# Attention scores in blocks of a triangle, one rescaling for the last rows, and a new list of shifts, in a fused scan and two-layer kernel

## The chip, the core and the metric

The kernel runs on one core of one Trainium2 chip, in one launch. The metric is device time in microseconds (us), from the start of the program to its end; smaller is better. TensorE is PE in the rows, with PEld for its weight loads; VectorE is DVE, ScalarE is ACT, GpSimd is POOL, and SyncE (SP) issues most of the DMA transfers.

## What is computed

The inputs x, a, B and C have 4 batches, 8 heads and 768 positions; a head has 32 values and a state of 16. A decayed linear attention goes first, cut to what matters:

```python
log_a = np.log(np.clip(a, 1e-06, 1.0))
for c in range(nc):                                # chunks of positions
    cum = np.cumsum(la, axis=-1)
    L = np.exp(cum[:, :, :, None] - cum[:, :, None, :]) * causal
    M = np.einsum('bhin,bhjn->bhij', Cc, Bc) * L   # scores, lower triangle
    y = M @ xc + (Cc @ state) * exp(cum)
    state = decay_full * state + sum_j (Bc_j x xc_j) * decay_from_j
```

Its 3072 rows of 256 values then pass two layers, each `h = x @ w_in` (256 to 2048), a function of h, and `g @ w_out` (2048 to 256). The first layer's function is ELU, the second's is Mish. All is float32.

## The kernel before

**Tiles.** The kernel takes chunks of T = 96 positions, not the reference's 32. With 8 chunks and 4 batches there are 32 tiles of the attention, numbered i = 4 x chunk + batch. A tile's scores for its 8 heads are 96x96 matrices with j on the partitions and i on the columns, so what counts is j up to i, and the rest is set to zero by the decay matrix `d` that they are multiplied with.

**Scores.** Tiles 0 to 7 (`TR0 = range(8)`) go the first way: C and B are transposed on TensorE in float32 (`at_tr0`, L699, four transposes), copied out, and multiplied in float32 by `at_scores0` (L739, 16 rows deep); one tile has eight of these matmuls in two blocks. Later tiles go the second way: ACT and DVE split B and C into three bfloat16 parts each (`at_split_1` to `at_split_4`, L610 to L627), one DMA transposes them (`at_split_5`, L631), and `at_scores` (L753) does one 96x96x96 matmul a head, four heads in each of two PSUM banks of the tag "s". `at_p` (L759) multiplies each bank into `d`. `at_y` (L791) then multiplies by x, head by head into 32 PSUM partitions each, two tiles at a time, and `at_st` (L828) makes the state's increment.

**Layers.** The rows are cut into blocks of 256 to 512 (`BL`), and each layer's 2048 inner values into 16 pieces. To hold float32 precision each product is made of three matmuls of high and low parts: L873 to L875 for h, L936 to L938 and L967 to L969 for the outputs. The first pieces of layer one use L941. The very last block of layer two (`LAST`) has its rows as PSUM partitions: `emit_y2` makes, for each group k of 128 rows, a matmul of 512 columns (L1006: the high part of g with high and low weights, in two halves of the bank) and one of 256 (L1007: the low part with the high weights, into half 0). `y2_out1` (L1022) scales half 1 into the result, `y2_out2` (L1027) scales half 0 and adds it, and `y2_store` (L1040) stores, part from SP's queue and part from ACT's.

**Weights.** The weights come as float64, in 32 loads of 512 KB; `job_1` to `job_5` (L391 to L434) make each into the high and low parts that the matmuls take.

**What sets the order.** The code does not issue instructions where it stands. Each piece is a `step` with one or more engines, a cost in us, and what it depends on. `run_steps` plans them all: it works a latest start for each step back from deadlines, adds to it what the table `SHIFT` has under the step's number, and then takes, engine by engine, the ready step with the earliest latest start. The instructions are emitted in the order so planned, and each engine runs its own list in that order. PSUM banks and other buffers are rings; `take` hands out the next place in one and notes who must be done with it.

Of the kernel before, what the change touches and what calls it, by code (L numbers as in the profile page):

```python
# [7 lines left out]
F32 = mybir.dt.float32  # L8
# [5 lines left out]
ALU = mybir.AluOpType  # L14
# [4 lines left out]
def tile_chain(  # L19
# [12 lines left out]
    nc = tc.nc  # L32
# [11 lines left out]
    DFF = w_in1.shape[1]  # L44
    NF = DFF // 128
    FP = 2
    EARLY = 10.0
    NP = NF // FP
    LAG = 5
    N0 = 8  # L50
    TR0 = range(8)

    ROWS = dict(zip(range(1, 4), (12, 13, 14, 15, 12, 14, 15)))
    WB, GB, HB, ND = 3, 3, 2, 3
# [32 lines left out]
    def early(step_k, cost):  # L87
# [2 lines left out]


    SHIFT = {
# [6 lines left out]
    }  # L99

    lock = set()
# [647 lines left out]
    def at_scores(i, half):  # L749
        s = s_t[i, half] = px.tile([T, H // 2, T], F32, tag="s", name="s")  # L750
        for k in range(H // 2):
# [2 lines left out]
                out=s[:, k, :], lhsT=bct[i, "b"][0:T, h, :], rhs=bct[i, "c"][0:T, h, :], start=True, stop=True  # L754
            )

    def at_p(i, half):
        hs = slice(half * (H // 2), (half + 1) * (H // 2))
        nc.vector.tensor_tensor(  # L759
            out=d_t[i][0:T, hs, :], in0=s_t.pop((i, half)), in1=d_t[i][0:T, hs, :], op=ALU.mult  # L760
        )
# [234 lines left out]
    def emit_y2(s, k):  # L996
        f = s % NF
        if f == 0:
            p, t = (pa, "acc") if k < 2 else (px, "s")
            acc[2, LAST, k] = p.tile([128, 2, DM], F32, tag=t, name="acc")  # L1000
        _, _, gh, gl = st[s]
        w = wt["o2", f // FP]
        y = acc[2, LAST, k]
        ts = slice(k * 128, k * 128 + 128)
        yk = y.rearrange("p z (k e) -> p z k e", k=2)
        nc.tensor.matmul(out=yk, lhsT=gh[:, ts], rhs=w[:, :, :, f % FP, :], start=(f == 0), stop=False)  # L1006
        nc.tensor.matmul(  # L1007
            out=yk[:, 0], lhsT=gl[:, ts], rhs=w[:, 0, :, f % FP, :], start=False, stop=(f == NF - 1)
        )
# [4 lines left out]
    def y2_out1(k, eng):  # L1014
        if k % 2 == 0:
            tl["oo", k] = at.tile([128, 2, DM], F32, tag="x", name="o", bufs=3)
        o = tl["o", k] = tl["oo", k - k % 2][:, k % 2]
        a, b = in_rows(acc[2, LAST, k][:, 1], o)
        if eng == V:
            nc.vector.tensor_scalar_mul(b, a, 1.0 / WS)  # L1020
        else:
            nc.scalar.activation(out=b, in_=a, func=AF.Copy, scale=1.0 / WS)  # L1022
# [72 lines left out]
    for j, (key, k) in enumerate(jobs):  # L1095
        rn, pn = [], []
        if j >= NJ:
            rn, pn = (w_free[j + 1 - NJ] if j + 1 < 2 * NJ else []), w_free[j - NJ]
            rf = []
            if j + 1 < 2 * NJ:  # L1100
                w_free[j + 1 - NJ] = rf
        else:
            rf = w_free[j]
            if key == "o1":
                w0_free[k] = rf
        q0 = step((DQ, 0.58, lambda j=j: load_job(j), 1.75), rn, rows_f.get(j, []))
        q1 = step(alt(lambda e, j=j: job_1(j, e), (V, 0.335), (A, 0.557)), q0)
        lock.add(q1)
        q2 = step((A, 0.552, lambda j=j: job_2(j)), q0)
        table[q2] = "exp"  # L1110
        q3 = step((V, 0.602, lambda j=j: job_3(j)), q1, q2)
        lock.add(q3)
        q4 = step(alt(lambda e, j=j: job_4(j, e), (A, 0.558), (V, 0.335)), q3, pn)
        q5 = step(alt(lambda e, j=j: job_5(j, e), (G, 1.27), (V, 0.603)), q4,
                  dl=slot_time(order.index((2, 0)) * NF + k * FP) + 10.0 if j >= NJ else 1e9)
        lock.update((q4, q5))
        rf.append(q5)
        raw_f = rf
        w_ready[key, k] = [q4, q5]
        LW.append(q0)  # L1120
        if key == "o1":
            w_ready["o0", k] = [q3]
# [56 lines left out]

    def two_scores(i, a5, tf, ex):  # L1180
        pz = []
        two = [take("s") for _ in range(2)]
        sc = step((PE, 0.43, lambda: [at_scores(i, z) for z in range(2)]), a5, [n for _, n in two])
        tf.append(sc)
        for z in range(2):
            pz.append(step((V, 0.47, lambda z=z: at_p(i, z)), sc, ex[z]))
            two[z][0].append(pz[-1])
        return pz
# [68 lines left out]
    for i in range(NB, tiles):  # L1257
        c, b = divmod(i, NB)
        if i % 2 == 0:
            bcf, bcn = take("bc")  # L1260
            lb = step((DQ, 1.15, lambda i=i: load_bc(i), 1.4), bcn)
            ys_dep, d_of = [], []
        d_f, d_n = take("d")
        d_of.append(d_f)
        if i in ROWS:
            lc, ex = rows_steps(i, d_n)
        else:
            lc = step((DQ, 0.52, lambda i=i: at_cumrow(i), 1.2), s_q4[c], d_n)
        cold = i in TR0
        if cold:  # L1270
            pf, pn = take("s")
            tr = step((PE, 0.40, lambda i=i: at_tr0(i)), lb, pn)
            tf, tn = take("t")
            a2 = step(alt(lambda e, i=i: at_tr0_out(i, e), (A, 0.372), (V, 0.47)), tr, tn)
            pf.append(a2)
        else:
            a2, a5, tf = three_parts(i, lb)
        if i not in ROWS:
            mk = step((G, 0.85, lambda i=i: at_mask(i)), lc)
            dd = []  # L1280
            for g in range(2):
                f = lambda e, i=i, g=g: at_diff(i, g * H // 2, (g + 1) * H // 2, e)
                dd.append(step(alt(f, (G, 0.80), (V, 0.47)), mk, s_q6))
                lock.add(dd[-1])
            ex = step((A, 0.735, lambda i=i: at_exp(i)), dd)
            table[ex] = "exp"
            ex = [ex, ex]
        csf, csn = take("cs")
        cs = step((G, 0.372, lambda i=i: at_cs(i)), lb, csn, s_d4)
        rc = step((V, 0.97, lambda i=i: at_rc(i)), cs, lc)  # L1290
        csf.append(rc)
        rc2 = step(alt(lambda e, i=i: at_rc2(i, e), (V, 0.37), (A, 0.52)), rc)
        lock.add(rc2)
        bcf += [a2, cs]
        if c + 1 < NCH:
            bf, bn = take("bw")
            b1 = step((G, 0.372, lambda i=i: at_bw_1(i)), lb, s_d3, bn)
            b2 = step((G, 0.372, lambda i=i: at_bw_2(i)), s_d7, b1)
            bcf.append(b1)
            ys_dep += [b1, b2]  # L1300
            d_of.append(bf)
        if cold:
            pz = []
            for z in range(2):
                two = [take("s"), take("s")]
                sc = step((PE, 0.52, lambda i=i, z=z: at_scores0(i, [z])), a2, [n for _, n in two])
                tf.append(sc)
                pz.append(step((V, 0.535, lambda i=i, z=z: at_p0(i, z)), sc, ex[z]))
                for pf, _ in two:
                    pf.append(pz[-1])  # L1310
        else:
            pz = two_scores(i, a5, tf, ex)
        ys_dep += [pz, rc, rc2]
        if i % 2 == 0:
            continue
        i -= 1
        pf, pn = take("s")
        parts, cost = [lambda i=i: at_y(i, 2)], 1.0
        if c + 1 < NCH:
            parts.append(lambda i=i: at_st(i))  # L1320
            cost = 1.2
        y = step((PE, cost, lambda parts=parts: [f() for f in parts]), ys_dep, LX[i], pn, SO[i - NB])
        oy = out_of_y(i, 2, y)
        if c + 1 < NCH:

            SO[i] = step((V, 1.2, lambda i=i: at_st_out(i)), y, LX[i + NB], list(YHI[i].values()))
            pf.append(SO[i])
        for f in d_of:
            f.append(y)
        pf += oy  # L1330
        xf[i].append(y)
# [93 lines left out]
    for f, k in [(f, k) for f in range(NF - 2) for k in range(NK)] + [(f, k) for k in range(NK) for f in (NF - 2, NF - 1)]:  # L1425
        s, ydep, gf, lf, ydl = last[f]
        y = step((PE, 0.347, lambda s=s, k=k: emit_y2(s, k)), ydep, four[k][1] if f == 0 else [], y, dl=ydl)
        gf.append(y)
        lf.append(y)
        if f == NF - 1:  # L1430
            if k % 2 == 0:
                _, on = take("x")
            o = step(alt(lambda e, k=k: y2_out1(k, e), (A, 0.27), (V, 0.33)), y, on)
            o = step((V, 0.35, lambda k=k: y2_out2(k)), o)
            step((DQ, 1.0, lambda k=k: y2_store(k), 0.48), o)
    run_steps()

# [29 lines left out]
```

## Time and profile before

| | us |
|---|---|
| median of three timed runs | 598.0 (597.68 to 598.23) |
| the profiled execution | 597.4 |
| its span, first to last instruction | 595.7 |
| PE busy | 585.2 |
| DVE busy | 427.6 |
| ACT busy | 363.2 |
| POOL busy | 133.1 |

The span is what lies between the first and the last instruction that the profiler recorded; the execution's own time has the launch's ends besides. Busy times are those of one execution, and an engine that is busy is not for that reason the one that others wait for; which one that is, the chain of waits tells, followed back from the last instruction. A matmul's row shows when it started and a modelled length that is longer than the step to the next one, since matmuls overlap: costs on PE are read from starts.

### The profile page before, as it was taken

To read this page: it belongs to the slowest core of one execution; us is meant where nothing else is said; L and a number is where in the kernel's file an instruction comes from. 1 tells how busy PE (TensorE), PEld (TensorE's weight loads), DVE (VectorE), ACT (ScalarE), POOL (GpSimd) and SP (SyncE) were. 2 spreads that over 40 slices of the span, in tenths; PEclk is the share of its full clock that TensorE was granted. 3 is DMA by queue.
4 is the path that set the end of the run, shared out by engine and by line. 5 is a ranking of instruction groups with operands and counts; after the bars stand their busy time and mean duration, and the time that the engine had idled before them with its cause. 6 is when DMAs were issued, how large, how long until landed. Compare 5 with 4: busy or idle time off the path is not lost.

```text
span 595.7 us, 10184 instructions
## 1 busy us (share of the span) xinstructions
PE 585.2 (98%) x3648; PEld 490.1 (82%) x3648; DVE 427.6 (72%) x941; ACT 363.2 (61%) x668; POOL 133.1 (22%) x200
## 2 busy tenths in 40 slices
PE   6999999999999999999999999999999999999997
PEld 5777999998888888888888788888888888888885
DVE  5898989999737889988776878665655665443443
ACT  4799999987615887777456796544543444322321
POOL 2455564340201245352005233000020000000000
PEclk9599999999999999999999999999999999999999
DMA  7999899310113656651015451100310000000101
GB/s 147 237 254 240 206 295 247 80 28 2 14 22 67 111 104 121 127 113 12 0 28 100 71 110 27 29 8 3 72 28 1 22 15 1 1 0 1 35 2 36
DMA packets 136279, 44.86 MB, mean 75 GB/s; under 512 B 124820, under 2 KB 125332, under 8 KB 136228
## 3 DMA queue, kind: packets, MB, share of 16 engines
q1 hardware_dynamic: 135876, 43.92, 33.7%
q8 instruction: 28, 0.46, 0.3%
q10 hardware_dynamic: 352, 0.30, 0.2%
q14 instruction: 23, 0.19, 0.1%
HBM read 31.48 MB, written 3.29 MB: 58 GB/s over the span
## 4 chain that ended last, share of the span: by engine, by line
PE 95%; DMA 2%; SPq 1%; DVE 1%; issue 0%; ACT 0%; POOL 0%; DVEq 0%; POOLq 0%
PE h L873 15%; PE h L874 15%; PE h L875 15%; PE acc L936 7%; PE acc L937 7%; PE acc L938 7%; PE acc L967 6%; PE acc L968 6%; PE acc L969 6%; PE acc L1006 3%; PE ys L791 2%; PE acc L941 2%; PE s L753 1%; PE acc L1007 1%; DMA t<-stk 1%; PE s L739 1%
## 5 line engine op out<-in xcount | busy, mean ns | idle before, releaser
L873 PE MATMUL h<-xyh,wi 128*128 128x512 f32 (+2 forms) x416 | 159.9, 384 | 0.0
L874 PE MATMUL h<-xyl,wi 128*128 128x512 f32 (+2 forms) x416 | 156.3, 376 | 0.0
L875 PE MATMUL h<-xyh,wi 128*128 128x512 f32 (+2 forms) x416 | 155.9, 375 | 0.0
L916 DVE TENSOR_TENSOR gl<-w,gh 128x512 fp32r<-128x512 f32 (+2 forms) x179 | 121.1, 678 | 21.8 <-ACT gh L417 13.2
L920 ACT ACTIVATE w<-h 128x512 f32<-128x512 f32 x96 | 57.0, 598 | 111.7 <-PE h L875 93.4
L419 DVE CAST gh<-w 128x512 fp32r<-128x512 f32 (+2 forms) x102 | 42.7, 419 | 75.6 <-PE acc L968 45.0
L873 PEld LDWEIGHTS h<-xyh,wi 128*128 128x128 f32 x416 | 78.9, 190 | 14.0 <-DVE g L905 0.3
L875 PEld LDWEIGHTS h<-xyh,wi 128*128 128x128 f32 x416 | 78.9, 190 | 12.9
L874 PEld LDWEIGHTS h<-xyl,wi 128*128 128x128 f32 x416 | 79.0, 190 | 11.8 <-DVE xyl L811 0.4
L889 ACT ACTIVATE w<-h 128x512 f32<-128x512 f32 (+2 forms) x104 | 55.9, 545 | 43.7 <-PE h L875 28.9
L936 PE MATMUL acc<-gh,wo 128*128 128x512 f32 (+2 forms) x208 | 75.8, 364 | 0.0
L937 PE MATMUL acc<-gh,wo 128*128 128x512 f32 (+2 forms) x208 | 74.9, 360 | 0.0
L938 PE MATMUL acc<-gl,wo 128*128 128x512 f32 (+2 forms) x208 | 74.9, 360 | 0.0
L417 ACT ACTIVATE gh<-w 128x512 fp32r<-128x512 f32 (+2 forms) x98 | 57.5, 592 | 27.5 <-PE acc L937 21.0
L967 PE MATMUL acc<-gh,wo 128*128 128x512 f32 x160 | 62.9, 393 | 0.0
L968 PE MATMUL acc<-gh,wo 128*128 128x512 f32 x160 | 62.3, 389 | 0.0
L969 PE MATMUL acc<-gl,wo 128*128 128x512 f32 x160 | 62.3, 389 | 0.0
L916 POOL TENSOR_TENSOR gl<-w,gh 128x512 fp32r<-128x512 f32 (+2 forms) x21 | 23.3, 1110 | 146.8 <-PE s L753 97.0
L897 DVE TENSOR_SCALAR w<-w 128x512 f32<-128x512 f32 (+2 forms) x71 | 28.6, 407 | 29.5 <-ACT w L889 29.2
L905 DVE TENSOR_TENSOR w<-h,w 128x512 f32<-128x512 f32 (+2 forms) x71 | 44.1, 626 | 1.6
L936 PEld LDWEIGHTS acc<-gh,wo 128*128 128x128 f32 x208 | 39.2, 188 | 5.5
L937 PEld LDWEIGHTS acc<-gh,wo 128*128 128x128 f32 x208 | 39.2, 188 | 5.1
(119 smaller groups left out, 865.5 us busy)
## 6 DMA issues: line engine op xcount, KB each, us to landing
raw<-in_moe_w_in_dram SPq DMA_DIRECT2D x16, 512.0 KB
raw<-in_moe_w_out_dram SPq DMA_DIRECT2D x16, 512.0 KB
d<-cum_d SPq DMA_DIRECT2D x28, 288.0 KB
xs<-in_x_dram SPq DMA_DIRECT2D x14, 192.0 KB
out_dram<-turned SPq DMA_DIRECT2D x80, 32.0 KB
bc<-in_C_dram SPq DMA_DIRECT2D x14, 96.0 KB
bc<-in_B_dram SPq DMA_DIRECT2D x14, 96.0 KB
xs<-in_x_dram SPq DMA_DIRECT2D x4, 96.0 KB
```

The source lines that it names most:

```text
L417: nc.scalar.activation(out=out, in_=in_, func=AF.Copy)
L873: nc.tensor.matmul(out=h, lhsT=hi[:, k, fs], rhs=xh[:, k, :], start=(k == 0), stop=False)
L874: nc.tensor.matmul(out=h, lhsT=hi[:, k, fs], rhs=xl[:, k, :], start=False, stop=False)
L875: nc.tensor.matmul(out=h, lhsT=lo[:, k, fs], rhs=xh[:, k, :], start=False, stop=(k == 1))
L916: alu(eng).tensor_tensor(out=gl, in0=w, in1=gh.bitcast(F32), op=ALU.subtract)
L920: nc.scalar.activation(out=new_w(s), in_=st[s][0], func=AF.Mish)
L936: nc.tensor.matmul(out=y, lhsT=hi[:, f % FP, ds], rhs=gh, start=(f == 0), stop=False)
L937: nc.tensor.matmul(out=y, lhsT=lo[:, f % FP, ds], rhs=gh, start=False, stop=False)
L938: nc.tensor.matmul(out=y, lhsT=hi[:, f % FP, ds], rhs=gl, start=False, stop=(f == NF - 1))
L967: nc.tensor.matmul(out=y, lhsT=hi[:, k], rhs=gh, start=(f == 0), stop=False)
L968: nc.tensor.matmul(out=y, lhsT=lo[:, k], rhs=gh, start=False, stop=False)
L969: nc.tensor.matmul(out=y, lhsT=hi[:, k], rhs=gl, start=False, stop=(f == NF - 1))
```

## The change

**Scores.** From tile 12 on (`TRI = 12`) `two_scores` calls `at_scores_tri` and `at_p_tri`. A head's 96x96 block is cut into its first 64 rows, with all 96 columns (`low`), and its last 32 rows with the last 32 columns (`high`); the piece that is left out lies wholly on the masked side. The low pieces of heads 0 to 4 go to PSUM partitions 0 to 63, which are the first half of the array's columns, and those of heads 5 to 7 to partitions 64 to 127; the high pieces go to partitions 64 to 95 (heads 0 to 3) and 96 to 127 (heads 4 to 7). All 16 pieces lie in one bank. DVE multiplies them into `d` in four instructions. The planner's cost for the matmuls is 0.33, and 0.74 and 0.56 for the products.

**Tile 7** goes the second way (`TR0 = range(7)`).

**The last 128 rows** (k = 3) sum everything into half 0: the matmul of 512 columns becomes two of 256 columns, and `y2_out1` alone scales the result.

**The plan.** `SHIFT` is a new list of 66 entries, the steps' numbers having moved; the deadline of the attention's low parts (`EARLY`) and of the last weight step are other, and so are the planned lengths of two kinds of transfer.

```diff
-    EARLY = 10.0
+    EARLY = 4.0
-    TR0 = range(8)
+    TR0 = range(7)
+    TRI = 12
...
     SHIFT = {
-        27: -2, 99: -1.5, 100: -3, 101: -5.5, 117: -9, 120: 6, 124: 4, 144: 4.5, 179: -4.5, 201: 3, 227: 5,
+        4: 1.5, 74: 2.5, 85: 1, 102: 7.5, 105: -1.5, 114: -15.5, 141: 14, 153: -10.5, 172: 16.5, 178: -5.5,
...
+    def at_scores_tri(i):
+        s = s_t[i] = px.tile([128, 512], F32, tag="s", name="s")
+        bt, ct = bct[i, "b"], bct[i, "c"]
+        def low(h):
+            q, n = (0, h * T) if h < 5 else (64, (h - 5) * T)
+            nc.tensor.matmul(
+                out=s[q:q + 64, n:n + T], lhsT=bt[0:T, h, 0:64], rhs=ct[0:T, h, :], start=True, stop=True
+            )
+        def high(h):
+            q, n = 64 + 32 * (h // 4), 3 * T + 32 * (h % 4)
+            nc.tensor.matmul(
+                out=s[q:q + 32, n:n + 32], lhsT=bt[0:T, h, 64:T], rhs=ct[0:T, h, 64:T], start=True, stop=True
+            )
+        for h in (0, 5, 1, 6, 2, 7, 3):
+            low(h)
+        for h in (0, 4, 1, 5):
+            high(h)
+        low(4)
+        for h in (2, 6, 3, 7):
+            high(h)
+    def at_p_tri(i, z):
+        s, r = s_t[i], d_t[i]
+        hs, q = (slice(0, 5), 0) if z == 0 else (slice(5, H), 64)
+        n = hs.stop - hs.start
+        d = r[0:64, hs, :]
+        nc.vector.tensor_tensor(
+            out=d, in0=s[q:q + 64, 0:n * T].rearrange("p (h s) -> p h s", h=n), in1=d, op=ALU.mult
+        )
+        d = r[64:T, 4 * z:4 * z + 4, 64:T]
+        q = 64 + 32 * z
+        nc.vector.tensor_tensor(
+            out=d, in0=s[q:q + 32, 3 * T:3 * T + 128].rearrange("p (h s) -> p h s", h=4), in1=d, op=ALU.mult
+        )
...
-        nc.tensor.matmul(out=yk, lhsT=gh[:, ts], rhs=w[:, :, :, f % FP, :], start=(f == 0), stop=False)
+        if k == NK - 1:
+            for z in range(2):
+                nc.tensor.matmul(
+                    out=yk[:, 0], lhsT=gh[:, ts], rhs=w[:, z, :, f % FP, :], start=(f == 0 and z == 0), stop=False
+                )
+        else:
+            nc.tensor.matmul(out=yk, lhsT=gh[:, ts], rhs=w[:, :, :, f % FP, :], start=(f == 0), stop=False)
...
+        if i >= TRI:
+            pf, pn = take("s")
+            sc = step((PE, 0.33, lambda: at_scores_tri(i)), a5, pn)
+            tf.append(sc)
+            for z in range(2):
+                pz.append(step((V, 0.74 if z == 0 else 0.56, lambda z=z: at_p_tri(i, z)), sc, ex))
+            pf += pz
+            return pz
...
-            lb = step((DQ, 1.15, lambda i=i: load_bc(i), 1.4), bcn)
+            lb = step((DQ, 1.15, lambda i=i: load_bc(i), 1.5), bcn)
...
-            lc = step((DQ, 0.52, lambda i=i: at_cumrow(i), 1.2), s_q4[c], d_n)
+            lc = step((DQ, 0.52, lambda i=i: at_cumrow(i), 1.7), s_q4[c], d_n)
...
-            o = step((V, 0.35, lambda k=k: y2_out2(k)), o)
+            if k < NK - 1:
+                o = step((V, 0.35, lambda k=k: y2_out2(k)), o)
```

The new functions move the lines behind them: L873 of before is L916 of the changed kernel, L409 is L411, L747 is L749, L811 is L854.

On PE, a tile's scores before, from the last big matmul ahead of them (`t` holds the transposed B and C, `s` is the bank); five more heads follow like these:

```order
L875 MATMUL h<-xyh,wi_1644 128x512
L753 LDWEIGHTS t
L753 MATMUL s<-t 96x96
L753 LDWEIGHTS t
L753 MATMUL s<-t 96x96
```

And now, in the middle of the block of tile 12, from the sixth 64-row piece to the second of the last four 32-row pieces:

```order
L767 MATMUL s<-t 64x96
L767 LDWEIGHTS t
L767 MATMUL s<-t 64x96
L773 LDWEIGHTS t
L773 MATMUL s<-t 32x32
L773 LDWEIGHTS t
L773 MATMUL s<-t 32x32
L773 LDWEIGHTS t
L773 MATMUL s<-t 32x32
L773 LDWEIGHTS t
L773 MATMUL s<-t 32x32
L767 LDWEIGHTS t
```

Pieces of two widths take turns on the same half of the array; a block has three such changes between its first and its last piece.

On DVE, between the products of the first tile and the last low part (`xyl`) that the first big matmuls wait for, before (`raw` are weights as loaded, `wi` weights made ready):

```order
L393 TENSOR_SCALAR raw_268<-raw_268 128x512
L409 SCALAR_TENSOR_TENSOR raw_268<-raw_268 128x512
L434 TENSOR_TENSOR wi_356<-raw_249,wi_356 128x512
L747 TENSOR_TENSOR d<-s,d 96x192 x2
L811 SCALAR_TENSOR_TENSOR xyl<-ys,xyh 128x2x96
L747 TENSOR_TENSOR d<-s,d 96x192 x2
L393 TENSOR_SCALAR raw_339<-raw_339 128x512
L409 SCALAR_TENSOR_TENSOR raw_339<-raw_339 128x512
L811 SCALAR_TENSOR_TENSOR xyl<-ys,xyh 128x2x96
```

And now:

```order
L395 TENSOR_SCALAR raw_291<-raw_291 128x512
L749 TENSOR_TENSOR d<-s,d 96x192 x2
L854 SCALAR_TENSOR_TENSOR xyl<-ys,xyh 128x2x96
L749 TENSOR_TENSOR d<-s,d 96x192 x2
L411 SCALAR_TENSOR_TENSOR raw_291<-raw_291 128x512
L854 SCALAR_TENSOR_TENSOR xyl<-ys,xyh 128x2x96
```

One weight piece fewer is made ready ahead of the last low part.

On PE, the end of the program now, the last group of 128 rows (`gh` and `gl` are the parts of the second layer's inner values):

```order
L1056 MATMUL acc<-wo_2283,gh 128x512
L1057 MATMUL acc<-wo_2283,gl 128x256
L1052 MATMUL acc<-wo_2283,gh 128x256 x2
L1057 MATMUL acc<-wo_2283,gl 128x256
L1052 MATMUL acc<-wo_2283,gh 128x256 x2
L1057 MATMUL acc<-wo_2283,gl 128x256
```

Where pairs of L1006 and L1007 stood to the end, each of the last two is now three matmuls of 256 columns.

## Rows read from the trace of the kernel before

**Rows 1.** The page: busy us (share) x instructions, and the chain's shares.

```profile
PE 585.2 (98%) x3648; PEld 490.1 (82%) x3648; DVE 427.6 (72%) x941; ACT 363.2 (61%) x668; POOL 133.1 (22%) x200
...
PE 95%; DMA 2%; SPq 1%; DVE 1%; issue 0%; ACT 0%; POOL 0%; DVEq 0%; POOLq 0%
```

**Rows 2.** Stretches: us, busy of PE, PEld, DVE, ACT, POOL, granted clock, DMA share, GB/s.

```profile
13.20:30.00 16.80, 16.26 (x162) 12.44 (x163) 13.30 (x34) 12.20 (x25) 7.88 (x11) 0.50 0.98 246
...
60.00:170.00 110.00, 110.00 (x792) 101.88 (x792) 97.38 (x230) 93.88 (x200) 41.73 (x60) 1.00 0.47 118
```

**Rows 3.** Timeline of PE: start us, length, line, operation, operands; cadence and score block.

```profile
299.66 0.39 PE L938 MATMUL acc<-gl,wo 128*128 128x512 f32 x1
...
306.00 0.52 PE L753 MATMUL s<-t 96*96 96x96 bf16 x8
...
306.66 0.39 PE L874 MATMUL h<-xyl,wi 128*128 128x512 f32 x1
```

**Rows 4.** Timeline of PE: a block of y and the state.

```profile
318.92 0.39 PE L875 MATMUL h<-xyh,wi 128*128 128x512 f32 x1
319.24 0.87 PE L791 MATMUL ys<-d,xs 128*32 128x96 f32 x32
319.93 0.41 PE L828 MATMUL ys<-xs,bw 128*32 128x64 f32 x16
...
320.60 0.40 PE L937 MATMUL acc<-gh,wo 128*128 128x512 f32 x1
```

**Rows 5.** Timeline of PE: tile 7's transposes and its second block of scores.

```profile
54.45 0.49 PE L699 MATMUL p_tr<-ident,bc 96*112 96x96 f32 x4
54.78 1.49 PE L941 MATMUL acc<-g,raw 128*128 128x384 f32 x4
...
59.78 0.34 PE L875 MATMUL h<-xyh,wi 128*128 128x384 f32 x1
60.05 0.58 PE L739 MATMUL s<-f32t 16*96 16x96 f32 x8
...
60.84 0.34 PE L937 MATMUL acc<-gh,wo 128*128 128x384 f32 x1
```

**Rows 6.** Timeline of PE at the start, at half clock.

```profile
16.53 0.55 PE L791 MATMUL ys<-d,xs 96*32 96x96 f32 x8
17.00 0.97 PE L739 MATMUL s<-f32t 16*96 16x96 f32 x16
...
18.73 0.87 PE L791 MATMUL ys<-d,xs 96*32 96x96 f32 x16
19.52 0.79 PE L538 MATMUL p_rd<-rows 6*96 6x96 bf16 x7
```

**Rows 7.** Groups of DVE by line: count | busy us, mean ns | idle before, releaser.

```profile
L759 DVE TENSOR_TENSOR d<-s,d 96x384 f32<-96x384 f32 x48 | 24.7, 547 | 3.2 <-PE s L753 3.0
L409 DVE SCALAR_TENSOR_TENSOR raw<-raw 128x512 int32<-128x512 int32 x32 | 21.9, 689 | 2.0 <-ACT raw L391 0.7 <-ACT raw L402 0.6 <-ACT xyh L805 0.5
L615 DVE TENSOR_TENSOR r<-bc,stk 96x128 f32<-96x128 f32 x44 | 12.3, 305 | 4.1 <-ACT stk L610 3.1
L393 DVE TENSOR_SCALAR raw<-raw 128x512 int32<-128x512 int32 x5 | 2.5, 509 | 0.1
```

**Rows 8.** Timeline of the end: the last matmuls but two, and DVE's last work.

```profile
590.78 0.28 PE L1007 MATMUL acc<-wo,gl 128*128 128x256 f32 x1
590.90 0.40 PE L1006 MATMUL acc<-wo,gh 128*128 128x512 f32 x1
...
591.87 0.49 DVE L1027 SCALAR_TENSOR_TENSOR o<-acc,o 128x128 f32<-128x128 f32 x2 [0.20 <-ACT o L1022]
```

**Rows 9.** Timeline of the start: the last masks, and the first big matmul.

```profile
21.34 1.34 POOL L547 TENSOR_SCALAR_AFFINE_SELECT d<-d 96x384 f32<-96x384 f32 x2 [3.40 <-DVE raw L409]
...
25.05 0.69 PE L873 MATMUL h<-xyh,wi 128*128 128x384 f32 x1
```

**Rows 10.** Timeline of PE: the one wait for a transposed tile.

```profile
342.12 0.56 PE L753 MATMUL s<-t 96*96 96x96 bf16 x8 [0.28 <-DMA t<-stk]
```

More of the change, by code (lines that the diff above doesn't have):

```diff
@@ L1017, in y2_out1 @@
         o = tl["o", k] = tl["oo", k - k % 2][:, k % 2]
-        a, b = in_rows(acc[2, LAST, k][:, 1], o)
+        a, b = in_rows(acc[2, LAST, k][:, int(k < NK - 1)], o)
         if eng == V:
@@ L1114, in tile_chain @@
         q5 = step(alt(lambda e, j=j: job_5(j, e), (G, 1.27), (V, 0.603)), q4,
-                  dl=slot_time(order.index((2, 0)) * NF + k * FP) + 10.0 if j >= NJ else 1e9)
+                  dl=slot_time(order.index((2, 0)) * NF + k * FP) + 25.0 if j >= NJ else 1e9)
         lock.update((q4, q5))
```

11 rows, old and new, of the table SHIFT are left out of this document.

## The prediction

> **What bounds the kernel now.** I read the busy times and the chain of work first, then the stretches, then single places. TensorE (PE) is busy 98% of the 595.7 us span, and the chain that ended last is PE for 95% of it [rows 1]. So what the change does to PE's own list decides, and work on DVE, ACT or POOL costs only where PE then waits. Between 60 and 170 us PE is busy 110.00 of 110 us while DVE is at 97.4 of 110; from 13.2 to 30 us it runs at half clock, and there alone it waits for others [rows 2]. The profiled execution took 597.4 us, 1.7 more than its span; the median of the three timed runs is 598.0. I make the sum as a difference and add it to 598.0.
>
> The unit of account is the cadence of the big matmuls: 28 of 512 columns start between 299.66 and 306.00, so 0.227 us each [rows 3]. What a small block costs is the time it pushes the next big one back. A block of eight score matmuls (L753) starts at 306.00, and the second big one behind it at 306.66: 0.66 less one cadence is **0.43 us**. Eight times 96 columns take about 0.35 of it (0.044 each), and 0.08 is the way back to big weights [rows 3].
>
> **Scores by parts of columns, tiles 12 to 31: 20 tiles.** Out go 20 blocks of 0.43 us. In come 20 blocks of sixteen matmuls: eight with 64 outputs and 96 columns, eight with 32 outputs and 32 columns, in the order seven, four, one, four. Left and right half of the array can run beside each other, so the streaming is that of the fuller half: five times 0.044, **0.22 us**.
>
> No block in the trace is cut into halves of 64; the nearest are the y blocks (L791, L828), which use quarters of 32. There 32 pieces of 96 columns follow each other in 0.69 us, 0.022 each [rows 4], while the same columns cost 0.08 each with the whole array (four transposes from 54.45 to 54.78 [rows 5]): parts do run beside each other, four at a time. But going into parts has a price. From 318.92 the first y matmul starts 0.32 later and not 0.23, so 0.09 is lost before anything streams; the whole block pushes the big ones back by 1.68 less two cadences, 1.23 us [rows 4]. Streaming explains 32 x 0.08 / 4 + 16 x 0.055 / 4 = 0.86, so 0.37 is entry, way back and weights; the whole-array block has 0.08 of that. **Entering and leaving cost 0.25 to 0.29 together.** This isn't peculiar to parts by columns: a block with the array cut by rows (L739, 59.78 to 60.84 [rows 5]) also starts 0.27 behind a matmul that takes 0.17.
>
> So a new block costs 0.22 + 0.08 + 0.25 = 0.55 us if nothing is lost between halves and quarters: 0.12 more than before, 20 times, **+2.4 us**. I take this value. The ends are far apart. Below: if halves cost nothing to enter, 0.30 us a block, -2.6 us. Above: if each change between halves and quarters drains the array as entering does. There are three more of them in a block, at 0.12 each (half of entry and way back), and the halves then no longer run beside the quarters (0.06): 0.97 us a block, +10.8 us. The only change from one kind of parts to another that the trace shows is from column parts to row parts: eight y pieces and the step to L739 take 0.47 (16.53 to 17.00), sixteen and the step to L538 0.79 (18.73 to 19.52), so eight pieces take 0.32 and the step 0.15, at half clock [rows 6]. That one drains. Both halves and quarters are parts by columns, with all rows, which is why I hold it likelier that a 32-wide part behind a 64-wide one goes like one quarter behind another.
>
> The Trainium skill speaks against me here: "TensorEngine Tiling (Array Packing)", section Key Properties, says that changing the tiling mode, and not just the tile, drains TensorE, and its list of configurations has 128x64 and 128x32 as separate ones. By that rule the step costs what the upper end above has; rows 4 to 6 agree with a drain on every change of kind that they hold, and none holds this change.
>
> DVE pays for the new shape too: its two products of 96x384 (547 ns [rows 7]) become four, of 480, 128, 288 and 128 columns. From 305 ns at 128 columns (L615) and 547 at 384 [rows 7] a column is 0.95 ns and an instruction 0.18 us, so 1.70 us a tile and not 1.09, 12 us in all. It lies beside PE: DVE is busy 72% of the span [rows 1] and 89% before 170 us [rows 2], so it has room later, where these tiles stand; and the y block that needs the products stands some matmuls behind. I cost it at nothing; if a y block waited for it, 0.5 us each time. One bank a tile and not two can only free PSUM sooner.
>
> **Tile 7 leaves the first path.** PE loses its four transposes (54.45 to 54.78, 0.33) and two blocks L739 (59.78 to 60.84 is 1.06 less two cadences of 0.17: 0.71 each) and gains one score block of 0.43 [rows 3, 5]: 0.33 + 1.42 - 0.43 = **-1.3 us**. ACT gains four passes for one, DVE four of 0.3 [rows 7], and SP one transpose ahead of weight loads, in a stretch where DVE and ACT are nearly full [rows 2]. PE never waited there, so I cost this at nothing; if that cover is gone, DVE's 1.2 us come back.
>
> **The last 128 rows in one scaling.** After the last matmul stands an ACT pass, then DVE with 0.49 us behind a hop of 0.20 [rows 8]; DVE's part goes, the store leaves right after ACT, but ACT's queue now issues the store of the rows before it first. I take **-0.4 us** (bounds -0.7 and 0). Sixteen matmuls of 512 columns become 32 of 256: a 256-column one takes 0.12 (590.78 to 590.90 [rows 8]), so two are 0.24 for 0.23 to 0.24, at most +0.2 us in all, which I count as +0.1.
>
> **The list planned anew.** Ahead of the first big matmul DVE has two L393 and one L409 less (0.5 and 0.69 us [rows 7]), and POOL makes its six masks in one go, where one now waits 3.40 us behind DVE and PE starts big work at 25.05 [rows 9]. That is up to 1.7 us of DVE time, but rows and masks also hold the start. I take **-0.5 us**, from -2 (the clock, at half until 30 us, rises with it) to +1. Later PE waited once for a transposed tile, 0.28 us at 342.12 [rows 10]; the new list may drop that wait or make others: **-0.2 us**, -0.3 to +1.
>
> **Sum:** +2.4 - 1.3 - 0.3 - 0.5 - 0.2 = +0.1 us, **598.1 us**: no change that can be measured. About 0.2% (1.2 us) is what a measurement of this kernel can tell from none.
>
> **Rivals.**
> 1. *Each change between halves and quarters drains.* +10.8 for +2.4: 606.5 us, slower by 1.4%. It decides from 0.13 us a block on over my 0.55 (then +2.6 us). For it: every change of kind in the rows costs 0.09 to 0.15 us. Against it: quarters behind quarters cost nothing, and all of these are column parts.
> 2. *Halves cost nothing to enter and the streaming is all.* -2.6 for +2.4: 593.1 us, faster by 0.8%. For it: nothing in the trace is 64 wide and in bf16 at full clock. Against it: both kinds of parts that are there pay on entry and on the way back.
> 3. *The start decides.* If the first big matmul comes 1.7 us sooner and the clock rises sooner with it, another -1.5 us: 596.4 us, faster by 0.3%. Against it: the chain there passes rows, exp, mask and product of tile 3 whatever DVE does between.
>
> **How the numbers follow.** My case 0.37, drain at each change 0.32, no price 0.19, the start 0.12. My case alone spans 596 to 600.2 (block 0.50 to 0.62, start and waits): faster 0.07, same 0.24, slower 0.06. The drain gives slower 0.32; no price faster 0.19; the start faster 0.09 and same 0.03. Together faster 0.35, same 0.27, slower 0.38. The range runs from 593.5 to 606.8: it leaves out somewhat over half of the no-price case, whose middle is 593.1, and the upper end of the drains.
>
> **What would show it.** In the profile of the changed kernel: the second big matmul behind a block of 64x96 and 32x32 matmuls starts 0.78 us after the block's first (0.55 and a cadence) in my case, 1.2 with drains, 0.53 with no price; between a 64-wide matmul and the 32-wide one behind it there are some 10 ns, or about 100. Tile 7 shows one block of 0.43 at some 60 us in place of the last two 16x96 ones. The last store leaves 0.4 to 0.5 us sooner behind the last matmul. PE starts big work before 25 us, or not. I am wrong above all if halves and quarters don't mix freely, and next if the stretch from 30 to 130 us shows PE waiting for weights or for the transposed tile 7.

## The result and the profile after

The changed kernel takes **606.56 us** (median of 4 runs, 605.9 to 606.8) beside 597.97 us for the kernel before in the same session: a ratio of 1.0138, 95% interval 1.012 to 1.0155. It is slower by 8.6 us. The forecast was 598.1, no change; what came is rival 1, a price at each change between halves and quarters, which had been put at 606.5. That the time still lies in the stated range, 593.5 to 606.8, by 0.24 us is due to the width of the range, which took in most of this rival. The profiled execution took 606.62 us, its span is 604.9.

The page of the changed kernel, the lines that answer to [rows 1], and its stretches, which answer to [rows 2] (columns as there):

```profile
PE 594.8 (98%) x3812; PEld 493.4 (82%) x3812; DVE 433.2 (72%) x962; ACT 370.1 (61%) x682; POOL 139.9 (23%) x208
...
PE 96%; ACT 2%; DVE 1%; issue 0%; DMA 0%
```

```profile
13.20:30.00 16.80, 16.58 (x160) 12.96 (x159) 13.58 (x35) 11.96 (x25) 6.29 (x10) 0.50 0.94 253
...
60.00:170.00 110.00, 109.58 (x780) 100.68 (x779) 99.08 (x232) 100.03 (x207) 42.07 (x58) 1.00 0.51 125
170.00:450.00 280.00, 280.00 (x1827) 224.05 (x1826) 207.17 (x461) 170.85 (x298) 68.50 (x102) 1.00 0.33 60
```

PE is still the bound, and it is busier: 594.8 us for 585.2. Nothing new waits between 170 and 450 us, where PE is busy all of the 280 us; so the time there has gone into PE's own list. One of the new blocks of scores, to hold against [rows 3] (timeline of PE in the changed kernel: start us, length, line, operation, operands):

```profile
221.71 0.39 PE L1012 MATMUL acc<-gl,wo 128*128 128x512 f32 x1
222.03 0.36 PE L767 MATMUL s<-t 96*64 96x96 bf16 x7
222.31 0.22 PE L773 MATMUL s<-t 96*32 96x32 bf16 x4
222.46 0.23 PE L767 MATMUL s<-t 96*64 96x96 bf16 x1
222.62 0.22 PE L773 MATMUL s<-t 96*32 96x32 bf16 x4
222.77 0.50 PE L916 MATMUL h<-xyh,wi 128*128 128x512 f32 x1
223.10 0.40 PE L917 MATMUL h<-xyl,wi 128*128 128x512 f32 x1
223.34 0.39 PE L918 MATMUL h<-xyh,wi 128*128 128x512 f32 x1
```

All blocks below are counted by one rule: from the start of the last big matmul before the block to the start of the third one behind it, less three cadences of 0.2267 (0.680 us). Here the starts, 221.71 and 223.34, are 1.635 us apart in full figures, so the block costs **0.955 us**. By the same rule a block before costs 1.108 - 0.680 = 0.428. Nineteen of the twenty new blocks stand between big matmuls; 16 of them are at 0.955, two 11 ns below it, and one at 354.86, whose transposed tile comes late, is 0.04 longer. The twentieth stands right behind a y block and adds 0.735.

What a change of width looks like is seen on the weight loads (timeline of PEld; first the block at 306.00 of the kernel before, then the one above of the changed kernel):

```profile
305.78 0.62 PEld L753 LDWEIGHTS <-t 96*96 96x96 bf16 x8
```

```profile
222.02 0.22 PEld L767 LDWEIGHTS <-t 96*64 96x64 bf16 x7 [0.35 <-issue]
222.31 0.12 PEld L773 LDWEIGHTS <-t 96*32 96x32 bf16 x4
222.46 0.11 PEld L767 LDWEIGHTS <-t 96*64 96x64 bf16 x1
222.62 0.11 PEld L773 LDWEIGHTS <-t 96*32 96x32 bf16 x4
222.77 0.19 PEld L916 LDWEIGHTS h<-xyh,wi 128*128 128x128 f32 x1
```

Before, the weights of the first score load from 305.78, 0.22 us ahead of the matmul at 306.00, under the big matmul. In the new block every load behind a change of width starts in the same 10 ns as its own matmul: 222.02 and 222.03, then 222.31, 222.46, 222.62 and 222.77 for both. Within one width the loads do run ahead: by single starts the seventh 64-wide load starts at 222.135 and its matmul at 222.176. So at each change there is no load ahead, where elsewhere there is one; what holds it back is not seen here.

The account of the span, 604.9 against 595.7, by the places where the traces differ:

| | us |
|---|---|
| scores: 19 x (0.955 - 0.428) + (0.735 - 0.428) | +10.3 |
| tile 7, one whole block in place of transposes and two 16x96 blocks | -1.3 |
| start: first big matmul at 24.57, before 25.05 | -0.5 |
| the wait of [rows 10], at 342.12: 0.04 of it left, at 354.86 | -0.45 |
| stalls of PE between 60 and 130 us: 1.5, before 0.2 | +1.3 |
| matmuls of the last 128 rows, 0.006 more in each group of four | +0.1 |
| from the last matmul's start to the end: 4.71, before 4.54 | +0.2 |
| sum (measured: +9.2) | +9.65 |

The 0.45 left over is not assigned.

### The profile page after: what moved, and what is told of

Its sections match the earlier page's. It is cut to its first block, busy times and chain, and to the rows that moved or that the text cites. A ratio compares the mean times of both kernels' runs of the same rounds, so it can differ in the third digit from the quotient of the medians.

```text
span 604.9 us, 10597 instructions
## 1 busy us (share of the span) xinstructions
PE 594.8 (98%) x3812; PEld 493.4 (82%) x3812; DVE 433.2 (72%) x962; ACT 370.1 (61%) x682; POOL 139.9 (23%) x208
## 4 chain that ended last, share of the span: by engine, by line
PE 96%; ACT 2%; DVE 1%; issue 0%; DMA 0%
PE h L916 15%; PE h L917 14%; PE h L918 14%; PE acc L979 7%; PE acc L980 7%; PE acc L981 6%; PE acc L1010 6%; PE acc L1011 6%; PE acc L1012 6%; PE ys L834 2%; PE acc L1056 2%; PE acc L984 2%; PE s L767 1%; PE acc L1057 1%; PE s L741 1%; PE s L773 1%
## 5 line engine op out<-in xcount | busy, mean ns | idle before, releaser
L916 PE MATMUL h<-xyh,wi 128*128 128x512 f32 (+2 forms) x416 | 160.3, 385 | 0.4 <-DVE w L946 0.2
L959 DVE TENSOR_TENSOR gl<-w,gh 128x512 fp32r<-128x512 f32 (+2 forms) x173 | 118.0, 685 | 16.7 <-ACT gh L419 8.9
L916 PEld LDWEIGHTS h<-xyh,wi 128*128 128x128 f32 x416 | 79.0, 190 | 15.2 <-DVE w L946 0.9
L932 ACT ACTIVATE w<-h 128x512 f32<-128x512 f32 (+2 forms) x104 | 55.0, 538 | 40.4 <-PE h L918 30.0
L419 ACT ACTIVATE gh<-w 128x512 fp32r<-128x512 f32 (+2 forms) x100 | 58.3, 585 | 27.4 <-PE acc L980 17.6
L959 POOL TENSOR_TENSOR gl<-w,gh 128x512 fp32r<-128x512 f32 (+2 forms) x27 | 29.6, 1099 | 132.5 <-ACT gh L419 61.9
L940 DVE TENSOR_SCALAR w<-w 128x512 f32<-128x512 f32 (+2 forms) x63 | 25.2, 404 | 28.5 <-ACT w L932 28.3
L981 PEld LDWEIGHTS acc<-gl,wo 128*128 128x128 f32 x208 | 39.2, 188 | 5.1
```

What stands on the lines that cost most here:

```text
L419: nc.scalar.activation(out=out, in_=in_, func=AF.Copy)
L916: nc.tensor.matmul(out=h, lhsT=hi[:, k, fs], rhs=xh[:, k, :], start=(k == 0), stop=False)
L959: alu(eng).tensor_tensor(out=gl, in0=w, in1=gh.bitcast(F32), op=ALU.subtract)
L981: nc.tensor.matmul(out=y, lhsT=hi[:, f % FP, ds], rhs=gl, start=False, stop=(f == NF - 1))
```

## The experiments

Each is compared with the kernel before on the same chip, whose median lay between 598.25 and 598.48 us. In the expectations a block of the first two runs is put at 0.741 and 0.541; by the rule above they are 0.732 and 0.535.

**One inner change.** The pieces of the changed kernel in another order, all 64-wide ones first:

```diff
-        for h in (0, 5, 1, 6, 2, 7, 3):
+        for h in (0, 5, 1, 6, 2, 7, 3, 4):
             low(h)
-        for h in (0, 4, 1, 5):
-            high(h)
-        low(4)
-        for h in (2, 6, 3, 7):
+        for h in (0, 4, 1, 5, 2, 6, 3, 7):
             high(h)
```

> The changed kernel, but in a tile's score block all eight 64-row pieces come first and then all eight 32-row pieces: one change of width inside the block in place of three, nothing else. Theory A (each change between halves and quarters drains the array, some 0.1 us and the exposed weights): block 0.956 falls by about 0.24 to 0.70 to 0.74 us, 20 times -4.7 us, 601.9 us. Theory B (the changes are free and it is the 32-wide pieces themselves that are dear, by their number): block unchanged at 0.95, 606.5 us.

602.33 us, ratio 1.007 (1.0055 to 1.0085). The block is 0.732 (PE's timeline; 219.73 to 221.14 are 1.412 in full figures):

```profile
219.73 0.39 PE L1009 MATMUL acc<-gl,wo 128*128 128x512 f32 x1
220.05 0.40 PE L767 MATMUL s<-t 96*64 96x96 bf16 x8
220.38 0.27 PE L773 MATMUL s<-t 96*32 96x32 bf16 x8
...
221.14 0.40 PE L915 MATMUL h<-xyh,wi 128*128 128x512 f32 x1
```

Two changes fewer and the same sixteen matmuls: 0.223 less a block, 4.2 us less in all. In this trace the wait for the transposed tile is back, at 351.11, where a block starts 0.43 us late.

**Quarters alone.** Each 64-wide piece is issued as two 32-wide ones, so a block has 24 matmuls of one width:

```diff
-            nc.tensor.matmul(
-                out=s[q:q + 64, n:n + T], lhsT=bt[0:T, h, 0:64], rhs=ct[0:T, h, :], start=True, stop=True
-            )
+            for j in (0, 32):
+                nc.tensor.matmul(
+                    out=s[q + j:q + j + 32, n:n + T], lhsT=bt[0:T, h, j:j + 32], rhs=ct[0:T, h, :], start=True, stop=True
+                )
```

> The changed kernel, but each 64-row piece is made as two 32-row pieces beside each other, so that the whole score block is in quarters, as the y blocks are: 24 matmuls, the same bank layout and the same products on DVE, no change of width inside. Theory A: entry, way back and streaming of 0.2 us are left: 0.53 to 0.55 us a block, 20 times -0.41: 598.3 us. Theory B (price by the number of pieces): 24 pieces for 16, so 1.2 us or more a block, 611 us or more.

599.5 us, ratio 1.0015 (0.9989 to 1.0041); the block is 0.535 (220.43 to 221.64 are 1.215 in full figures):

```profile
220.43 0.39 PE L1013 MATMUL acc<-gl,wo 128*128 128x512 f32 x1
220.75 0.35 PE L768 MATMUL s<-t 96*32 96x96 bf16 x14
...
221.64 0.40 PE L919 MATMUL h<-xyh,wi 128*128 128x512 f32 x1
```

More matmuls, and 7 us less. The time is 1.2 us over the expected 598.3 although the block is as expected. In its trace the wait for the transposed tile is back (0.36 us late at 349.89), big work starts 0.38 us later than in the changed kernel (24.95), and the end is 0.33 us longer (5.04). This run takes away the halves together with the changes, so it can't tell a dear change from dear 64-wide pieces; the next does.

**Halves alone.** The last 32 rows of each head go through a 64-wide piece as well:

```diff
-            q, n = (0, h * T) if h < 5 else (64, (h - 5) * T)
+            q, n = 64 * (h // 4), h % 4 * T
...
-            q, n = 64 + 32 * (h // 4), 3 * T + 32 * (h % 4)
+            q, n = 64 * (h // 4), 4 * T + 32 * (h % 4)
             nc.tensor.matmul(
-                out=s[q:q + 32, n:n + 32], lhsT=bt[0:T, h, 64:T], rhs=ct[0:T, h, 64:T], start=True, stop=True
+                out=s[q:q + 64, n:n + 32], lhsT=bt[0:T, h, 32:T], rhs=ct[0:T, h, 64:T], start=True, stop=True
             )
...
```

The heads now lie four and four on the two halves, not five and three; all first pieces are issued before all second ones, and the products on DVE are cut to match.

> The changed kernel with one width in a block: the last 32 rows of a head's scores are computed by a 64-wide piece too (rows 32 to 95, of which the first 32 are not read), so a block is 16 matmuls, all 64 wide. Theory A, what costs is a change of width: no inner change is left, the block is at 0.50 to 0.56 us as with quarters alone (0.541), and the time at 606.5 - 20 x 0.42 = 598 us, between 597.5 and 599.5. The rival, the 64-wide pieces are dear by themselves (the run with quarters alone took them away along with the changes, so it could not tell): a block of 0.70 us or more and 601.5 us or more.

599.65 us, ratio 1.0017 (0.9997 to 1.0038), the block 0.606 (220.07 to 221.36 are 1.286 in full figures):

```profile
220.07 0.39 PE L1008 MATMUL acc<-gl,wo 128*128 128x512 f32 x1
220.39 0.36 PE L767 MATMUL s<-t 96*64 96x96 bf16 x8
...
221.36 0.40 PE L914 MATMUL h<-xyh,wi 128*128 128x512 f32 x1
```

That is 0.05 a block over the expected band and 0.15 us over the expected time, but far from the rival's 0.70: halves are not dear by themselves. Computing 32 rows too many with the same width is cheaper by 0.126 us a block than the right 32 rows with one change.

**Seven inner changes.** The same sixteen pieces, two halves and two quarters in turn:

```diff
-        for h in (0, 5, 1, 6, 2, 7, 3):
-            low(h)
-        for h in (0, 4, 1, 5):
-            high(h)
-        low(4)
-        for h in (2, 6, 3, 7):
-            high(h)
+        for hl, hh in (((0, 5), (0, 4)), ((1, 6), (1, 5)), ((2, 7), (2, 6)), ((3, 4), (3, 7))):
+            for h in hl:
+                low(h)
+            for h in hh:
+                high(h)
```

> The changed kernel with the same 16 matmuls in an order that goes back and forth: two 64-wide pieces, two 32-wide, four times, so seven inner changes rather than three. Theory A, each change of width has its price, 0.107 us by the steps from one inner change (0.741) to three (0.956): the block is at 0.956 + 4 x 0.107 = 1.38 us and the time at 606.5 + 20 x 0.43 = 615 us, between 613 and 617. The rival, a toll per block that more changes do not raise (weight loads waiting once): a block under 1.1 us and under 609.5 us.

615.73 us, ratio 1.0281 (1.0254 to 1.0308), the block 1.395. A block of it (timeline of PE, columns as above):

```profile
224.20 0.39 PE L1010 MATMUL acc<-gl,wo 128*128 128x512 f32 x1
224.52 0.23 PE L767 MATMUL s<-t 96*64 96x96 bf16 x2
224.68 0.19 PE L773 MATMUL s<-t 96*32 96x32 bf16 x2
224.81 0.23 PE L767 MATMUL s<-t 96*64 96x96 bf16 x2
224.97 0.19 PE L773 MATMUL s<-t 96*32 96x32 bf16 x2
...
226.28 0.39 PE L916 MATMUL h<-xyh,wi 128*128 128x512 f32 x1
```

Each pair of 64-wide pieces holds the next pair back by 0.16 us, each pair of 32-wide ones by 0.12 to 0.13, and the second pair of a kind pays like the first. The runs together:

| inner changes | kernel | block us | us per change | time us |
|---|---|---|---|---|
| 0 | halves alone | 0.606 | | 599.65 |
| 1 | all halves, then all quarters | 0.732 | 0.126 | 602.33 |
| 3 | the changed kernel | 0.955 | 0.112 | 606.56 |
| 7 | two by two | 1.395 | 0.110 | 615.73 |

From one change to seven the sixteen pieces are the same and only their order differs; the step from none to one also swaps eight 32-wide pieces for 64-wide ones. The price is per change and all but constant, **0.11 us**, from one change to seven. A toll per block that more changes do not raise is ruled out.

The one block of each kernel that stands right behind a y block bears this out. With quarters alone it adds 0.206 us there, 0.329 less than between big matmuls, so 0.329 is what entering and leaving cost. Behind the y block's quarters, a block that begins with 64-wide pieces saves the 0.329 and pays one more change: 0.955 - 0.329 + 0.11 = 0.736, measured 0.735; one inner change 0.513, measured 0.521; halves alone 0.387, measured 0.389; two by two 1.176, measured 1.169.

**The triangle alone.** The kernel before with its list and its eight tiles on the first path, and only the scores of tiles 12 to 31 as in the change:

```diff
     TR0 = range(8)
+    TRI = 12
...
```

> The kernel before with the triangle's scores alone: neither tile 7, nor the last evacuation, nor the re-planned list (the step numbers of the old one still fit). Theory A, the price is the block's own: a block holds up the stream of matmuls by 0.95 us as in the changed kernel (0.956 there, 0.432 before), 20 blocks, so 598.2 + 20 x 0.524 = 608.7 us, between 607.5 and 610. The rival, the price comes from where the new list puts the blocks: blocks of 0.85 us or less, and 606 us or less.

608.1 us, ratio 1.0154 (1.0129 to 1.0179), the block 0.955 again. The price belongs to the block, not to the new list. In this trace PE starts 1.0 us late in all between 60 and 130 us (0.81 of it at 115.67), and a block waits for its transposed tile at 258.92, 0.6 us late.

**All but the triangle.** The changed kernel with whole 96x96 blocks for every tile:

```diff
-    TRI = 12
+    TRI = 32
```

> The changed kernel with the triangle's blocks nowhere (TRI = 32): scores of tiles 7 to 31 in whole 96x96 blocks over two banks, as before; tile 7, the last rows and the list stay as changed. Theory A and B alike: 20 blocks of 0.956 become 0.432: -10.5 us, 596.1 us; then what is left of the change is worth -1.9 us against before, most of it tile 7's -1.3. If the blocks cost through DVE's products or through the plan, the gain is smaller and waits of PE on DVE stay.

597.6 us, ratio 0.9994 (0.997 to 1.0018): no difference, where 596.1 was expected. Tile 7's 1.3 us are there, but in its trace the starts of PE between 60 and 130 us come 2.4 us late in all, against 0.2 before. The traced execution is the fastest of the ten, 596.2 us, and its start is early: big work begins at 24.08, and between 28 and 30 us the granted clock is 0.99, so the upper of TensorE's two levels (2.4 GHz), where the kernel before still has 0.50, the lower (1.2 GHz); PE had been busy all of the 2 us ahead of that in both. The eighteenth big matmul starts at 29.39 there, at 30.77 before and at 30.37 in the changed kernel. So 1 us of what this trace gains on the changed kernel lies in its start. Two of the waits, in PE's timeline of that run and of the changed kernel (in brackets the idle time and its releaser):

```profile
119.72 0.39 PE L981 MATMUL acc<-gl,wo 128*128 128x256 f32 x1 [0.21 <-POOL gl L959]
```

```profile
75.11 0.34 PE L918 MATMUL h<-xyh,wi 128*128 128x384 f32 x1
75.69 0.45 PE L916 MATMUL h<-xyh,wi 128*128 128x384 f32 x1 [0.24 <-DVE w L946]
```

At 75.11 the next start is 0.58 us away and not 0.17. The matmul wants the bank that DVE's L946 frees, and that stands behind ACT (DVE's and ACT's timelines of the changed kernel):

```profile
75.08 0.55 DVE L946 SCALAR_TENSOR_TENSOR w<-w,h 128x384 f32<-128x384 f32 x1 [0.24 <-ACT w L938]
```

```profile
73.61 0.47 ACT L932 ACTIVATE w<-h 128x384 f32<-128x384 f32 x1
73.98 0.66 ACT L419 ACTIVATE wo<-raw 128x512 fp32r<-128x512 f32 x1
74.53 0.52 ACT L938 ACTIVATE w<-w 128x384 f32<-128x384 f32 x1
```

A weight conversion of 0.66 us (L419) runs between the two ACT passes of one slot, L932 and L938. The late starts behind the matmuls at 69.75, 75.11, 80.41 and 114.64 of the changed kernel come to 1.5 us; only the one at 75.11 is followed back here. That the four extra ACT passes and the DVE work of tile 7 are what tips them is not shown: no run changes tile 7 alone, since this would renumber the steps that the list's table shifts. And it can't be all, for the triangle alone and the last run below, both with the old list and with tile 7 on the first path, have 1.0 and 0.9 us of late starts in the same stretch.

**A store on the other queue.** The run above, with the second store of k = 2 on SP's queue instead of ACT's:

```diff
-            q = nc.scalar if p else nc.sync
+            q = nc.scalar if p and k != NK - 2 else nc.sync
```

> As e3_square, and the second store of group k = 2 of the last rows goes out on SP's queue and not on ACT's. Theory: the end was not set by DVE's adding but by two stores one behind the other on ACT's queue, 1.42 us from 600.75; with one of them there the last store leaves about 0.6 us sooner: 595.5 us, 0.6 below e3_square. Rival: the landing of the store sets the end whatever the queue, or SP's stores become the last: no difference, within 0.2 us.

597.96 us, ratio 0.9997 (0.9987 to 1.0006): no gain. The end of three kernels, before, changed and this one (timelines; ACTq and SPq are the DMA issues of these engines):

```profile
591.14 0.28 PE L1007 MATMUL acc<-wo,gl 128*128 128x256 f32 x1
...
591.74 1.43 ACTq L1040 DMA_DIRECT2D out_dram<-o  x2
```

```profile
600.15 0.28 PE L1057 MATMUL acc<-wo,gl 128*128 128x256 f32 x1
...
600.75 1.42 ACTq L1090 DMA_DIRECT2D out_dram<-o  x2
```

```profile
590.94 3.34 SPq L1090 DMA_DIRECT2D out_dram<-o  x5
...
591.77 0.28 PE L1057 MATMUL acc<-wo,gl 128*128 128x256 f32 x1
...
592.51 0.37 ACTq L1090 DMA_DIRECT2D out_dram<-o  x1
```

In both kernels ACT's queue issues two stores one behind the other, and the second is through 2.03 us after the last matmul's start before (591.74 + 1.43 - 591.14), 2.02 after. With one of them moved, ACT's queue is through at 592.88, 1.11 after; but SP now has five, and is through at 594.28, 2.51 after. Work has only moved from one queue to the other.

**Quarters behind quarters.** The one block of the quarters run that stands right behind a y block adds 1.446 - 1.240 = 0.206 us (both blocks by the rule above, and a y block alone). This run makes nine of them, from the kernel before: the first tile of each pair from 14 on has its scores in quarters, issued in the y step of the pair before.

```diff
...
+        if i in MERGE:
+            pf, pn = take("s")
+            parts, more, y = held_y[i]
+            more += [a5, pn]
+            parts.append(lambda: at_scores_tri(i))
+            sc = step((PE, 0.0, lambda: None), y)
...
-        y = step((PE, cost, lambda parts=parts: [f() for f in parts]), ys_dep, LX[i], pn, SO[i - NB])
+        more = []
+        if i + 2 in MERGE:
+            cost += 0.2
+        y = step((PE, cost, lambda parts=parts: [f() for f in parts]), ys_dep, LX[i], pn, SO[i - NB], more)
+        held_y[i + 2] = parts, more, y
```

> The kernel before, with its whole 96x96 scores and its list, but for the first tile of nine pairs (tiles 14, 16, ..., 30): their scores are quarters (32-wide pieces alone) and are issued right behind the y block of the pair before, which is quarters too. Theory A, a block pays for changes of width and for nothing else: behind a y block there is none on the way in, and the way out is the y block's own, so it adds what the one such case of the quarters run added (1.446 us for both against 1.240 for y alone, 0.206), 0.22 less than the 0.428 of a whole block. Nine times that is -2.0 us: 596.3 us beside a before of 598.3, between 595.3 and 597.3. The rival, the y blocks now stand later, and what waits for them takes the gain back: 0.206 each, but 598 us or more, with PE waiting behind the y blocks.

596.76 us (12 runs), before 598.44 (17 runs): ratio 0.9975, 0.9949 to 1.0001. It is faster than the changed kernel by 10 us; over the kernel before, 0.25% is likely, but the interval just reaches 1. The trace is clearer than the time: six of the nine joint blocks are at 1.445 or 1.446, two 6 and 14 ns longer, and the ninth, whose y block has 32 matmuls and not 48, adds 0.22. PE's timeline of one:

```profile
208.67 0.39 PE L1013 MATMUL acc<-gl,wo 128*128 128x512 f32 x1
208.99 0.87 PE L835 MATMUL ys<-d,xs 128*32 128x96 f32 x32
209.67 0.41 PE L872 MATMUL ys<-xs,bw 128*32 128x64 f32 x16
209.89 0.34 PE L768 MATMUL s<-t 96*32 96x96 bf16 x14
...
210.79 0.40 PE L919 MATMUL h<-xyh,wi 128*128 128x512 f32 x1
```

From 208.67 to 210.79 are 2.125 us in full figures. The scores follow the y block with no gap, and in the stretch from 170 to 450 us PE is busy 279.98 of 280: no wait of PE behind a later y block is seen. The span of this trace, 595.8 us, is no shorter than the 595.7 before: its first big matmul comes at 25.36, late starts follow between 60 and 130 us, and the end is 0.39 us longer. So the gain is read from the blocks and from the median of the twelve runs; the traced one took 597.49 us.

## Why the prediction was wrong, step by step

**The step that failed** is the one that the prediction argued last in the cost of a block: "Both halves and quarters are parts by columns, with all rows, which is why I hold it likelier that a 32-wide part behind a 64-wide one goes like one quarter behind another." It doesn't. Three inner changes cost 0.11 each, 20 blocks, 6.7 us of the 8.6. The single change of kind that [rows 6] held, 0.15 at half clock, had already pointed to this; the likeness of halves and quarters was set against it without any row of its own. The sign named for it was right: about 100 ns between a 64-wide matmul and the 32-wide one behind it. By single starts it is 136 ns (222.176 to 222.312), where two rounds of 64-wide pieces are 39 apart.

The Trainium skill, "TensorEngine Tiling (Array Packing)", says in its section Key Properties that a change of the tiling mode drains TensorE, and in its section Available Configurations it lists 128x64 and 128x32 as separate ones. The runs agree in so far as each of the changes counted here costs 0.11 us; that what happens there is a drain, no run shows.

**Entry and way back** were right in size. The prediction had 0.09 on entry and 0.25 to 0.29 for both together, where a whole block pays 0.08. At 221.71 the first piece starts 0.32 later and not 0.23, so 0.09; and the first two big matmuls behind the block start 0.34 apart and not 0.23. Both ways together were put at 0.08 + 0.25 = 0.33 and measured 0.329, the streaming at 0.22 and measured 0.206 in quarters. The block without inner changes was put at 0.55 and measured 0.535 in quarters and 0.606 in halves. The two runs that make this case real, one width and no inner change, took 599.5 and 599.65 us, some 1 us over before, and neither interval excludes no change. So that case was put about right; what was wrong was that the kernel is this case.

**Rival 1** was priced right: 0.97 a block for 0.955, 606.5 us for 606.56. In it 0.06 stood for halves that no longer run beside quarters, and its 0.12 per change was half of entry and way back; the runs put the change at 0.11. Its sign, 1.2 us from the block's first matmul to the second big one, was mis-stated: the entry lies ahead of the first matmul, and the distance, 222.03 to 223.10, is 1.08 in full figures. The 0.78 of the prediction's own case has the same fault (0.67 in quarters, 0.74 in halves). That the whole comes within 0.1 us of 606.5 is in part luck: the blocks cost 0.5 us less than this rival had, the list and the end 1.7 us more, and what is left over in the account and the scatter between runs take most of that back.

**DVE's four products** cost nothing on PE, as said. The two groups of DVE between 155 and 470 us (count | busy us, mean ns of one):

```profile
L791 DVE TENSOR_TENSOR d<-s,d 64x480 f32<-64x480 f32 (+1 forms) x40 | 22.1, 553 | 10.0 <-PE s L773 8.8 <-ACT d L651 0.6
...
L796 DVE TENSOR_TENSOR d<-s,d 32x128 f32<-32x128 f32 x40 | 11.7, 292 | 0.5
```

Twice 553 and twice 292 are 1.69 us a tile, forecast 1.70, and PE is busy all the time from 170 to 450 us.

**Tile 7** came as worked out on PE. One whole block stands where [rows 5] had the last two 16x96 ones (PE's timeline of the changed kernel):

```profile
58.09 0.34 PE L918 MATMUL h<-xyh,wi 128*128 128x384 f32 x1
58.27 0.52 PE L755 MATMUL s<-t 96*96 96x96 bf16 x8
...
59.04 0.34 PE L981 MATMUL acc<-gl,wo 128*128 128x384 f32 x1
```

59.04 less 58.09 is 0.95, less three cadences of 0.173 is 0.43. But "PE never waited there, so I cost this at nothing" was wrong about the cover: in that nearly full stretch new stalls of PE came up.

**The start** moved by the 0.5 us that were forecast, 24.57 for the 25.05 of [rows 9], but this is luck as much as foresight: the seven traces with the new list have their first big matmul between 23.97 and 25.25, the three with the old one between 24.81 and 25.36. Nor do POOL's six masks come in one go. Four start at 14.97, and two wait 3.90 us for DVE's L411 until 20.95, as two waited 3.40 before.

**The list planned anew** was put at -0.2 for its waits, within -0.3 and +1. Of the wait at 342.12 only 0.04 is left (-0.45), but the list has not removed it for good: with shorter blocks it stands again, 0.43 in the run with one inner change and 0.36 with quarters alone. And 1.3 us of stalls came between 60 and 130 us, so the term is +0.9. The prediction had named this stretch as the second place where it could be wrong.

**The last evacuation** was put at -0.4 and is worth nothing. DVE's 0.49 us are gone, but "ACT's queue now issues the store of the rows before it first", and that is the whole of it: the two issues take 1.42 us as before, and the last is through 2.02 us behind the last matmul for 2.03. The bound of 0 was right, the value taken wasn't.

## What to carry to other kernels

Count the changes of tile width in PE's stream before the streamed columns: here each cost a quarter of what a whole block cost, so a triangle that saved columns and added changes lost. Give small matmuls of one stretch one width, even at the price of rows computed for nothing or of more instructions; this alone only undid the loss here (599.5 and 599.65 us, before 598.25 and 598.48). What paid on PE was to put them behind a block that already has that width. At the end of a kernel, see which queue issues the last stores before shortening the work in front of them.

## What the runs showed of the hardware that was not expected

- A change between 64-wide and 32-wide pieces, all with 96 rows of bf16, costs 0.11 us, as near as much as going from whole-array matmuls into pieces (0.09). At each change the weight load starts together with its matmul and not ahead of it; whether the array is first emptied or the load is held for another reason, no run tells apart.
- Pieces of one width on different columns start 3 to 4 ns apart, and a block of 24 quarters behind a block of quarters costs 0.206 us, less than half of the eight whole-array matmuls for the same tile (0.428).
- Profiled runs of nearly the same program differ at their ends: the first big matmul came between 23.97 and 25.36 us, and the time from the last matmul's start to the end was 4.5 to 5.05 us. A difference of 0.5 us there between two single traces shows nothing of a change.
